# One copy of the K transposes addressed through a register, and PV in two column tiles of 64, in a one-core decode kernel

## The chip, the cores and the metric

The kernel runs on one core of one Trainium2 chip. The metric is the device time of one execution in microseconds. The kernel before takes 196.64 us, the median of three runs (196.57 to 196.75).

## The reference

Four sequences each decode one token. After a layer norm, the sum of three terms is written out: the input, an attention with its output projection, and a SwiGLU feed-forward.

```python
W = 4096                                   # the last 4096 positions of the cache
q = (xn @ wq), 32 heads of 128
k, v = the last W rows of 8 cached heads, each used by 4 query heads
scores = einsum("bhqd,bhkd->bhqk", q, k) * 128 ** -0.5
o = einsum("bhqk,bhkd->bhqd", softmax(scores), v) @ wo
out = x + o + (silu(xn @ w_gate) * (xn @ w_up)) @ w_down
```

There are 4 sequences, 8 cached heads, 16 query columns per cached head (4 sequences times 4 query heads), and 16384 rows of K and of V per cached head. One cached head of K, or of V, is 4 MB in bf16.

## The kernel before, in words

The work on the cache is a loop of eight passes, one per cached head, and a ninth, short one. K and V each have two buffers of 4 MB in SBUF, `KB[0]`, `KB[1]` and `VB[0]`, `VB[1]`; a head's parity chooses the buffer. A buffer holds 128 blocks of 128 by 128.

In pass j, TensorE does the following for head j-1.

- **Transposes** (`transposes`, line 415): 128 blocks of K are turned, eight to a PSUM bank and a group. The three banks `ps_kt0` to `ps_kt2` are used in turn. Each group (number n, 0 to 15) is copied to SBUF (`kT`) by VectorE (line 335, ten groups) or ScalarE (line 268, the groups 4, 7, 8, 11, 12 and 14). A group waits until the bank is free, which the semaphore `s_ev[n - 3]` tells.
- **Scores** (line 424): each turned block is the stationary operand, and 16 columns of q move through it. The results of all 128 blocks fill the four banks `ps_s`. The program goes: transposes 0 to 7, scores 0 to 3, transposes 8 to 11, scores 4 to 7, transposes 12 to 15, scores 8 to 15.
- **Sums of the previous head's exponentials** (line 515), then a transpose (line 519) of the column maxima that VectorE has reduced from the four banks (lines 339 to 365).
- **PV of the previous head** (`pv`, line 433): two blocks of the probabilities P (32 columns) are the stationary operand, and two blocks of V (256 columns) move. Four such products go to four column tiles of 32, that is, to four strips of 32 PSUM partitions in `ps_o`. Of each product only the two diagonal pieces of 16 by 128 are meant; the others are computed and left unused.
- **Shift** (line 532): four products subtract the maxima from the scores in place. ScalarE then takes the exponentials (line 271).
- **Fold** (line 536): VectorE has copied `ps_o` to SBUF (line 347), and fp32 products with a 0/1 matrix (`fold`) add the strips' pieces up. VectorE multiplies the result by the reciprocal of the sums (line 349) and so makes a head's output, and signals `s_nm`.

The maxima, the exponentials and the copies lie on VectorE and ScalarE, and the PV of a head runs one pass after its scores.

TensorE's program is a loop with branches. Three transposes sections and the PV section exist twice, once for each parity (`by_parity`), since the address of a K or V buffer is a constant in them. TensorE's sequencer (the part that reads the program) executes branches, register arithmetic and some waits itself and hands weight loads and products on to the array's queue. Where an address depends on a register, it is worked out by an instruction of its own, shown as FUSED_REGOPS in the profile and as ISA in the program's order. Before the change there is such an instruction at line 424, one ahead of each of three groups of scores, since all products of a group read the same q.

All transfers of K, V and the weights are issued by SyncE on one queue in a fixed order: the weights of q, gate and up, K0, K1, V0, then K2, V1, K3, V2 and so on to V7, then the weights of the down and output projections. The load of K for head r waits until the transposes of head r-2 are done (line 230, signal `s_tr[15]`), the load of V for head r until PV of pass r is done (line 235, signal `s_pv`).

After the ninth pass the tail (`t_tail`, line 554) transposes the heads' outputs, multiplies by the two projections' weights (lines 566, 574 and 586) and writes the result.

Of the kernel before, what the change touches and what calls it, by code (L numbers as in the profile page):

```python
# [3 lines left out]
BF16 = mybir.dt.bfloat16  # L4
FP32 = mybir.dt.float32
ALU = mybir.AluOpType
ACT = mybir.ActivationFunctionType
AX = mybir.AxisListType


def bass_parallel_sum__sliding_block_cached__swiglu_ffn__decode_kernel(
# [12 lines left out]
    B, _, D = A_x.shape  # L24
    _, HKV, Sk, Dh = A_k_cache.shape
# [6 lines left out]
    NT = W * B // 128  # L32
# [6 lines left out]
    CQ = B * REP  # L39
# [8 lines left out]

    sb = nc.alloc_sbuf_tensor
    sb("pad_to_512", [128, (-nc.sbuf_base) % 512 // 2], BF16)  # L50
    KB = [sb("kbuf%d" % s, [128, NT, Dh], BF16) for s in range(2)]
    VB = [sb("vbuf%d" % s, [128, NT, Dh], BF16) for s in range(2)]
    WG = sb("wg_sb", [128, NC, F], BF16)
    WU = sb("wu_sb", [128, NC, F], BF16)
    WD = WG[:].rearrange("p c n -> p (c n)").rearrange("p (t n) -> p t n", n=D)
    WO = KB[0][:].rearrange("p t d -> p (t d)").rearrange("p (j n) -> p j n", n=D)
    WQ = VB[1][:].rearrange("p t d -> p (t d)").rearrange("p (c n) -> p c n", c=NC)

    X = sb("x_sb", [B, D], BF16)
# [8 lines left out]
    P = sb("p", [128, NT, CQ], BF16)  # L68
# [8 lines left out]
    mask = sb("mask", [128, CQ], FP32)  # L77
    nrm = sb("nrm", [48, 1], FP32)
    Dsh = sb("dsh", [128, CQ], BF16)
    o4 = sb("o4", [128, 256], FP32)  # L80
    dsum = sb("dsum", [128, CQ], FP32)
    rden = sb("rden", [128, CQ], FP32)
    OT = sb("oT", [128, HKV + 1, CQ], BF16)
# [6 lines left out]
    ident = sb("ident", [128, 128], BF16)  # L90
# [2 lines left out]
    I48 = sb("i48", [48, CQ], FP32)  # L93
    Lsel = sb("lsel", [128, 128], BF16)
    fold = sb("fold", [128, 32], FP32)
    sel = sb("sel", [128, B, 128], BF16)
    quarter = sb("quarter", [128, 4], FP32)
    opf = sb("opf", [128, B, 32], FP32)
# [4 lines left out]
    ps_kt = [ps("ps_kt%d" % s, [128, 512], FP32) for s in range(3)]  # L103
    ps_O = ps("ps_o", [128, 512], FP32)
    kt_ps = [t[:].bitcast(BF16).rearrange("p (a b) -> p a b", b=128) for t in ps_kt]
    S_ps = [t[:].rearrange("p (t c) -> p t c", c=CQ) for t in ps_S]
    mx_ps = ps_kt[2][:, 0:128]
    mask_ps = ps_O[:, 0:CQ]
    o4_ps = ps_O[:, 0:256]
    dn_ps = ps_kt[0]  # L110
    ot_ps = ps_O[:, 288:288 + CQ]
    xT_ps = ps_S[0][:].bitcast(BF16)[:, 0:NC * B]
    gate_ps = ps_S[2]
    up_ps = ps_S[3]
# [11 lines left out]
    d_k = [sem("d_k%d" % g) for g in range(2)]  # L126
# [34 lines left out]
    s_oc = sem("s_oc")  # L161
    s_sl = sem("s_sl")
    s_nm = sem("s_nm")
# [20 lines left out]
    def kv_ap(cache, r):  # L184
        return cache[:, r, Sk - W:, :].rearrange("b (s t) d -> s b (t d)", t=NT)
# [41 lines left out]
    def run_sync(eng):  # L227
        def load_k(r):
            if r >= 2:
                eng.wait_ge(s_tr[NCH - 1], r - 1)  # L230
            eng.dma_start(KB[r % 2][:].rearrange("p t d -> p (t d)"), kv_ap(A_k_cache, r)).then_inc(d_k[r % 2], 16)

        def load_v(r):
            if r:
                eng.wait_ge(s_pv, r)
            eng.dma_start(VB[r % 2][:].rearrange("p t d -> p (t d)"), kv_ap(A_v_cache, r)).then_inc(d_v[r % 2], 16)

        eng.dma_start(WQ[:], wq_ap).then_inc(d_v[1], 16)
        eng.dma_start(WG[:], wg_ap).then_inc(d_wg, 16)
        eng.dma_start(WU[:], wu_ap).then_inc(d_wu, 16)  # L240
        load_k(0)
        load_k(1)
        load_v(0)
        for r in range(2, HKV):
            load_k(r)
            load_v(r - 1)
        load_v(HKV - 1)
        eng.dma_start(WD, wd_ap).then_inc(d_wd, 16)  # L248
        for q, (a, b) in enumerate(ROWS):
            if q == 0:  # L250
                eng.wait_ge(s_tr[NCH - 1], HKV - 1)
            eng.dma_start(WO[:, a:b, :], wo_ap[:, a:b, :]).then_inc(d_wo[q], 16)  # L252
        eng.wait_ge(s_y, 1)
        eng.dma_start(out_ap, y_ap).then_inc(d_out, 16)
        eng.wait_ge(d_out, 16)
# [20 lines left out]
    def run_vector(eng):  # L276
        me = bass.OrderedEngineSet([eng.engine])
        nx = nc.alloc_registers("v_r", engines=me)
# [23 lines left out]
        for h in (0, 32):  # L302
            eng.tensor_copy(I48[h:h + CQ, :], identf[h:h + CQ, h:h + CQ])
        eng.tensor_reduce(fold[:], ident[:].rearrange("p (g m) -> p m g", m=32), AX.X, ALU.add)
        eng.tensor_reduce(quarter[:], ident[:].rearrange("p (g m) -> p m g", m=4), AX.X, ALU.add)
        eng.tensor_copy(I4w[:].rearrange("p (b e) -> p b e", e=8)[:, :, 0], ident[0:B, 0:B])
        eng.wait_ge(s_q, 1)
# [33 lines left out]
        def sums(v, slot):  # L341
            eng.wait_ge(s_dn, v)
            eng.tensor_reduce(dsum[:], dn_ps[:].rearrange("p (t c) -> p c t", c=CQ), AX.X, ALU.add)  # L343
            eng.drain()
            eng.reciprocal(rden[:], dsum[:])
            eng.wait_ge(s_pv, v)
            eng.tensor_copy(o4[:], o4_ps).then_inc(s_oc, 1)  # L347
            eng.wait_ge(s_sl, v)
            eng.tensor_tensor(slot, ot_ps, rden[:], ALU.mult).then_inc(s_nm, 1)  # L349

# [33 lines left out]
        for q in range(1, 4):  # L384
            eng.drain()
            dst = opf[:] if q < 3 else OP[:].rearrange("p j (b e) -> p b j e", e=8)[:, :, :, 0]
            last = eng.scalar_tensor_tensor(dst, op_ps[:, :, q, :], quarter[:, q:q + 1], opf[:], ALU.mult, ALU.add)
# [6 lines left out]
    def run_tensor(eng):  # L394
        mm = eng.matmul
        me = bass.OrderedEngineSet([eng.engine])
# [4 lines left out]
        def now(reg, lo=1, hi=16 * HKV):  # L401
            return eng.snap(reg, min_val=lo, max_val=hi, donate=True)
# [1 line left out]
        def step(reg, by, op=ALU.add):  # L404
            nc.regs_alu(reg, reg, by, op=op)

        def transposes(g, a, b):
            if a == 0:
                eng.wait_ge(d_k[g], now(nk[g]))
            j = now(nx)  # L410
            for n in range(a, b):
                if n >= 3:
                    eng.wait_ge(s_ev[n - 3], j)
                for k in range(8):
                    last = eng.transpose(kt_ps[n % 3][:, k, :], KB[g][:, 8 * n + k, :], ident[:])  # L415
                last.then_inc(s_tr[n], 1)

        def scores(j, n):
# [9 lines left out]
                last.then_inc(s_sc[q], 1)  # L428

        def pv(e):  # L430
            for u in range(NT // 2):
                k = u % 4
                last = mm(o4_ps[32 * k:32 * k + 32, :], P[:, 2 * u:2 * u + 2, :].rearrange("p t c -> p (t c)"),  # L433
                          VB[e][:, 2 * u:2 * u + 2, :].rearrange("p t d -> p (t d)"),
                          start=(u < 4), stop=(u >= NT // 2 - 4), skip_group_check=True)
            last.then_inc(s_pv, 1)

        later = []
# [1 line left out]
        def by_parity(name, body):  # L440

            eng.br_lt(odd, 1, on_true=name + "_even", on_false=name + "_odd")
            later.append((name, body))
            with nc.body(name + "_even", valid_engines=me):
                body(0)
                nc.br(name + "_end", engines=me)
# [44 lines left out]

        with nc.body("t_pass", valid_engines=me):
            by_parity("t_a", lambda g: transposes(g, 0, 8))
        with nc.body("t_a_end", valid_engines=me):
            j = now(nx, 1, HKV)
            for n in range(0, 4):
                scores(j, n)
            by_parity("t_b", lambda g: transposes(g, 8, 12))  # L500
        with nc.body("t_b_end", valid_engines=me):
            j = now(nx, 1, HKV)
            for n in range(4, 8):
                scores(j, n)
            by_parity("t_c", lambda g: transposes(g, 12, 16))
        with nc.body("t_c_end", valid_engines=me):
            j = now(nx, 1, HKV)
            for n in range(8, 16):
                scores(j, n)
            nc.br("t_values", engines=me)  # L510
        with nc.body("t_values", valid_engines=me):
            j = now(nx)
            for q in range(NB):
                eng.wait_ge(s_xp[q], j)
                last = mm(dn_ps[:], ones[:], P[:, q * TB:(q + 1) * TB, :].rearrange("p t c -> p (t c)"),  # L515
                          start=(q == 0), stop=(q == NB - 1))
            last.then_inc(s_dn, 1)
            eng.wait_ge(s_cm, j)
            eng.transpose(mx_ps, mxd[:], identf[:]).then_inc(s_mt, 1)  # L519
            eng.wait_ge(s_nm, j)  # L520

            def turn(g):
                eng.wait_ge(d_v[1 - g], eng.snap(nk[g], min_val=16, max_val=16 * HKV))
                step(nk[g], 16)
                pv(1 - g)

            by_parity("t_p", turn)
        with nc.body("t_p_end", valid_engines=me):
            j = now(nx)
            eng.wait_ge(s_dd, j)  # L530
            for q in range(NB):
                mm(S_ps[q], Lsel[:], bc(Dsh[:], TB), start=False, stop=True,  # L532
                   skip_group_check=True).then_inc(s_sh[q], 1)
            eng.wait_ge(s_oc, j)
            for e in range(2):
                last = mm(ot_ps, o4[:, 128 * e:128 * e + 128], fold[:, 16 * e:16 * e + 16],  # L536
                          start=(e == 0), stop=(e == 1), skip_group_check=True)
            last.then_inc(s_sl, 1)
            nc.br("t_step", engines=me)
        with nc.body("t_step", valid_engines=me):  # L540
# [85 lines left out]
```

## Time and profile before

| what | value |
|---|---|
| median of three runs | 196.64 us |
| the profiled execution, whole | 196.87 us |
| its span in the profile | 195.4 us |
| PE busy (TensorE products) | 155.1 us (79%), 2903 instructions |
| PEld busy (weight loads) | 120.8 us (62%), 2912 |
| DVE (VectorE) busy | 115.3 us (59%), 220 |
| ACT (ScalarE) busy | 68.9 us (35%), 86 |
| packets of the main DMA queue | 97.1% of 16 engines' time, 81.01 MB |
| transposes, line 415 | 1024, busy 72.4 us |
| scores, line 424 | 1024, busy 29.4 us |
| PV, line 433 | 576, busy 18.8 us |

The span is what lies between the first and the last instruction of the execution; the whole has 1.5 us around it. The busy time of a group is the union of its instructions, so overlapping products count once. The "chain" goes back from the last instruction, at each step to what released it, and gives start, length, engine, tile and line. The "windows" give the busy time of each engine in a stretch and the clock that was granted to TensorE, 1.00 being full. PEldq marks what TensorE's sequencer executed itself; such instructions are not counted as busy.

### The profile page before, as it was taken

To read this page: it belongs to the slowest core of one execution; us is meant where nothing else is said; L and a number is where in the kernel's file an instruction comes from. 1 tells how busy PE (TensorE), PEld (TensorE's weight loads), DVE (VectorE), ACT (ScalarE), POOL (GpSimd) and SP (SyncE) were. 2 spreads that over 40 slices of the span, in tenths; PEclk is the share of its full clock that TensorE was granted. 3 is DMA by queue.
4 is the path that set the end of the run, shared out by engine and by line. 5 is a ranking of instruction groups with operands and counts; after the bars stand their busy time and mean duration, and the time that the engine had idled before them with its cause. 6 is when DMAs were issued, how large, how long until landed. Compare 5 with 4: busy or idle time off the path is not lost.

```text
span 195.4 us, 6505 instructions
## 1 busy us (share of the span) xinstructions
PE 155.1 (79%) x2903; PEld 120.8 (62%) x2912; DVE 115.3 (59%) x220; ACT 68.9 (35%) x86; POOL 9.2 (5%) x27
## 2 busy tenths in 40 slices
PE   0038935997999899899989989998699879987653
PEld 0012105985788679778867968886598758955311
DVE  5642373666486766758676676867276747672501
ACT  2003100470447056444706634560447046603001
POOL 7820000000000000000000000000000000000000
PEclk9999996698799999999999999999889999999968
DMA  6999999999999999999999999999999999999991
GB/s 216 429 438 432 459 429 436 433 429 426 426 429 426 429 431 436 443 429 429 436 429 429 429 429 429 429 429 429 436 429 436 429 436 429 429 429 398 419 401 52
DMA packets 3633, 81.09 MB, mean 415 GB/s; under 512 B 424, under 2 KB 556, under 8 KB 940
## 3 DMA queue, kind: packets, MB, share of 16 engines
q1 hardware_dynamic: 3620, 81.01, 97.1%
q8 instruction: 4, 0.07, 0.1%
q14 instruction: 1, 0.01, 0.0%
q10 hardware_dynamic: 8, 0.00, 0.0%
HBM read 81.01 MB, written 0.00 MB: 415 GB/s over the span
## 4 chain that ended last, share of the span: by engine, by line
DMA 45%; PE 39%; ACT 7%; DVE 3%; issue 2%; SPq 2%; DVEq 0%
DMA kbuf<-in_A_k_cache_dram 28%; PE ps_kt L415 21%; DMA kbuf<-in_A_wo_dram 17%; PE ps_s L424 9%; ACT kT L268 7%; PE ps_o L433 6%; PE ps_s L532 2%; DVE mxb L339 2%; PE ps_kt L519 1%; PE ps_o L536 1%; SPq L252 1%; DVE mx L362 1%; DVE mxd L364 0%; DVE kT L335 0%; SPq L248 0%
## 5 line engine op out<-in xcount | busy, mean ns | idle before, releaser
L415 PE MATMUL ps_kt<-ident,kbuf 128*128 128x128 bf16 x1024 | 72.4, 227 | 9.5 <-DMA kbuf<-in_A_k_cache_dram 5.9
L415 PEld LDWEIGHTS ps_kt<-ident,kbuf 128*128 128x128 bf16 x1024 | 61.9, 102 | 16.8 <-ACT kT L268 6.4
L335 DVE COPY kT<-ps_kt 128x1024 bf16<-128x1024 bf16 x80 | 52.2, 687 | 20.3 <-PE ps_kt L415 19.5
L268 ACT COPY kT<-ps_kt 128x1024 bf16<-128x1024 bf16 x48 | 47.8, 1013 | 44.5 <-PE ps_kt L415 44.5
L271 ACT ACTIVATE p<-ps_s 128x512 bf16<-128x512 f32 x32 | 16.5, 604 | 46.1 <-PE ps_s L532 46.1
L339 DVE TENSOR_REDUCE mxb<-ps_s 128x16 f32<-128x512 f32 x32 | 22.1, 692 | 13.3 <-PE ps_s L424 11.6
L424 PE MATMUL ps_s<-qT,kT 128*128 x1024 | 29.4, 169 | 0.0
L424 PEld LDWEIGHTS ps_s<-qT,kT 128*128 128x128 bf16 x1024 | 27.8, 96 | 0.3
L433 PE MATMUL ps_o<-vbuf,p 128*32 128x256 bf16 x576 | 18.8, 287 | 1.3 <-DMA vbuf<-in_A_v_cache_dram 0.8
L433 PEld LDWEIGHTS ps_o<-vbuf,p 128*32 128x32 bf16 x576 | 16.1, 101 | 4.2 <-issue 3.4
L532 PE MATMUL ps_s<-dsh,lsel 128*128 128x512 bf16 x36 | 9.4, 381 | 0.0
L515 PE MATMUL ps_kt<-p,ones 128*128 128x512 bf16 x27 | 7.6, 379 | 0.9 <-ACT p L271 0.2
L467 PE MATMUL ps_s<-vbuf,xnT 128*32 128x512 bf16 x32 | 3.6, 629 | 5.0 <-DMA vbuf<-in_A_wq_dram 5.0
L519 PE MATMUL ps_kt<-identf,mxd 128*128 128x128 f32 x9 | 3.0, 328 | 5.3 <-DVEq L365 5.3
L343 DVE TENSOR_REDUCE dsum<-ps_kt 128x16 f32<-128x512 f32 x9 | 6.2, 692 | 1.5 <-PE ps_kt L515 1.3
L349 DVE TENSOR_TENSOR oT<-ps_o,rden 128x16 f32 (+1 forms) x9 | 1.6, 175 | 8.9 <-PE ps_o L536 8.9
L519 PEld LDWEIGHTS ps_kt<-identf,mxd 128*128 128x128 f32 x9 | 1.3, 140 | 8.4 <-DVEq L365 8.4
L536 PEld LDWEIGHTS ps_o<-fold,o 128*128 128x128 f32 x36 | 5.4, 190 | 1.3
L347 DVE COPY o<-ps_o 128x256 f32<-128x256 f32 x9 | 3.8, 425 | 3.8 <-PE ps_o L433 3.2
L574 PE MATMUL ps_s<-kbuf,oP 128*32 128x512 bf16 x22 | 2.8, 623 | 3.8 <-DMA kbuf<-in_A_wo_dram 3.8
L457 PE MATMUL ps_s<-ident,xn 4*128 4x4 bf16 x4 | 0.3, 166 | 6.6 <-DVE xn L297 6.6
L274 ACT COPY part<-ps_s 64x512 f32<-64x512 f32 x1 | 0.6, 580 | 13.4 <-PE ps_s L574 13.4
(92 smaller groups left out, 71.7 us busy)
## 6 DMA issues: line engine op xcount, KB each, us to landing
kbuf<-in_A_k_cache_dram SPq DMA_DIRECT2D x8, 4096.0 KB, 24.3
vbuf<-in_A_v_cache_dram SPq DMA_DIRECT2D x8, 4096.0 KB, 26.2
vbuf<-in_A_wq_dram SPq DMA_DIRECT2D x1, 4096.0 KB, 12.1
kbuf<-in_A_wo_dram SPq DMA_DIRECT2D x1, 2048.0 KB, 29.9
wg_sb<-in_B_w_gate_dram SPq DMA_DIRECT2D x1, 1792.0 KB, 16.0
wu_sb<-in_B_w_up_dram SPq DMA_DIRECT2D x1, 1792.0 KB, 19.8
wg_sb<-in_B_w_down_dram SPq DMA_DIRECT2D x1, 1792.0 KB, 25.6
kbuf<-in_A_wo_dram SPq DMA_DIRECT2D x1, 896.0 KB, 33.0
```

The source lines that it names most:

```text
L268: eng.copy(KT[n % 8][:], kt_ps[n % 3]).then_inc(s_ev[n], 1)
L271: eng.activation(P[:, q * TB:(q + 1) * TB, :], S_ps[q], ACT.Exp, scale=SCALE).then_inc(s_xp[q], 1)
L335: eng.tensor_copy(KT[n % 8][:], kt_ps[n % 3]).then_inc(s_ev[n], 1)
L339: eng.tensor_reduce(mxb[:, q, :], S_ps[q].rearrange("p t c -> p c t"), AX.X, ALU.max)
L343: eng.tensor_reduce(dsum[:], dn_ps[:].rearrange("p (t c) -> p c t", c=CQ), AX.X, ALU.add)
L415: last = eng.transpose(kt_ps[n % 3][:, k, :], KB[g][:, 8 * n + k, :], ident[:])
L424: last = mm(S_ps[q][:, 8 * (n % 4) + k, :], KT[n % 8][:, k, :], QT[:, bass.ds(j, 1), :, :].rearrange("p o b h -> p (o b h)"), start=(n % 4 ...
L433: last = mm(o4_ps[32 * k:32 * k + 32, :], P[:, 2 * u:2 * u + 2, :].rearrange("p t c -> p (t c)"), VB[e][:, 2 * u:2 * u + 2, :].rearrange(" ...
L515: last = mm(dn_ps[:], ones[:], P[:, q * TB:(q + 1) * TB, :].rearrange("p t c -> p (t c)"), start=(q == 0), stop=(q == NB - 1))
L519: eng.transpose(mx_ps, mxd[:], identf[:]).then_inc(s_mt, 1)
L532: mm(S_ps[q], Lsel[:], bc(Dsh[:], TB), start=False, stop=True, skip_group_check=True).then_inc(s_sh[q], 1)
L536: last = mm(ot_ps, o4[:, 128 * e:128 * e + 128], fold[:, 16 * e:16 * e + 16], start=(e == 0), stop=(e == 1), skip_group_check=True)
```

## The change

K's two buffers become one tensor with an index 0 or 1, and the transposes stand once in the program. Each one's K address is worked out from the register `odd`, which changes between 0 and 1 at the end of each pass. Only the wait for K's arrival still exists for each parity. PV now takes four blocks of P (64 columns) as the stationary operand and four blocks of V (512 columns) as the moving one, alternating between two column tiles of 64 partitions. `ps_o` is therefore filled to its 512 columns, VectorE's copy of it is 512 wide, and the fold is four products with a new 0/1 matrix, `fold4`, instead of two. The fold's result moves from `ps_o` to a free part of `ps_kt2`. For that reason the third group of transposes now waits for `s_nm` (the product of VectorE that reads the fold's result), and the wait for `s_nm` stands ahead of the maxima's transpose instead of behind it.

```diff
-    KB = [sb("kbuf%d" % s, [128, NT, Dh], BF16) for s in range(2)]
+    KBA = sb("kbuf", [128, 2, NT, Dh], BF16)
+    KB = [KBA[:, s] for s in range(2)]
...
-    o4 = sb("o4", [128, 256], FP32)
+    o4 = sb("o4", [128, 512], FP32)
...
+    fold4 = sb("fold4", [128, 64], FP32)
...
-    o4_ps = ps_O[:, 0:256]
+    o4_ps = ps_O
...
-    ot_ps = ps_O[:, 288:288 + CQ]
+    ot_ps = ps_kt[2][:, 256:256 + CQ]
...
+        eng.tensor_reduce(fold4[:], ident[:].rearrange("p (g m) -> p m g", m=64), AX.X, ALU.add)
...
-        def transposes(g, a, b):
-            if a == 0:
-                eng.wait_ge(d_k[g], now(nk[g]))
+        def transposes(a, b):
             j = now(nx)
+            g = eng.snap(odd, min_val=0, max_val=1)
             for n in range(a, b):
+                if n == 2:
+                    eng.wait_ge(s_nm, j)
                 if n >= 3:
                     eng.wait_ge(s_ev[n - 3], j)
                 for k in range(8):
-                    last = eng.transpose(kt_ps[n % 3][:, k, :], KB[g][:, 8 * n + k, :], ident[:])
+                    last = eng.transpose(kt_ps[n % 3][:, k, :],
+                                         KBA[:, bass.ds(g, 1), 8 * n + k, :].rearrange("p o d -> p (o d)"), ident[:])
                 last.then_inc(s_tr[n], 1)
...
         def pv(e):
-            for u in range(NT // 2):
-                k = u % 4
-                last = mm(o4_ps[32 * k:32 * k + 32, :], P[:, 2 * u:2 * u + 2, :].rearrange("p t c -> p (t c)"),
-                          VB[e][:, 2 * u:2 * u + 2, :].rearrange("p t d -> p (t d)"),
-                          start=(u < 4), stop=(u >= NT // 2 - 4), skip_group_check=True)
+            for u in range(NT // 4):
+                k = u % 2
+                last = mm(o4_ps[64 * k:64 * k + 64, :], P[:, 4 * u:4 * u + 4, :].rearrange("p t c -> p (t c)"),
+                          VB[e][:, 4 * u:4 * u + 4, :].rearrange("p t d -> p (t d)"),
+                          start=(u < 2), stop=(u >= NT // 4 - 2), skip_group_check=True)
             last.then_inc(s_pv, 1)
...
         with nc.body("t_pass", valid_engines=me):
-            by_parity("t_a", lambda g: transposes(g, 0, 8))
-        with nc.body("t_a_end", valid_engines=me):
+            by_parity("t_k", lambda g: eng.wait_ge(d_k[g], now(nk[g])))
+        with nc.body("t_k_end", valid_engines=me):
+            transposes(0, 8)
             j = now(nx, 1, HKV)
             for n in range(0, 4):
                 scores(j, n)
-            by_parity("t_b", lambda g: transposes(g, 8, 12))
-        with nc.body("t_b_end", valid_engines=me):
-            j = now(nx, 1, HKV)
+            transposes(8, 12)
             for n in range(4, 8):
                 scores(j, n)
-            by_parity("t_c", lambda g: transposes(g, 12, 16))
-        with nc.body("t_c_end", valid_engines=me):
-            j = now(nx, 1, HKV)
+            transposes(12, 16)
             for n in range(8, 16):
                 scores(j, n)
...
+            eng.wait_ge(s_nm, j)
             eng.wait_ge(s_cm, j)
             eng.transpose(mx_ps, mxd[:], identf[:]).then_inc(s_mt, 1)
-            eng.wait_ge(s_nm, j)
...
-            for e in range(2):
-                last = mm(ot_ps, o4[:, 128 * e:128 * e + 128], fold[:, 16 * e:16 * e + 16],
-                          start=(e == 0), stop=(e == 1), skip_group_check=True)
+            for e in range(4):
+                last = mm(ot_ps, o4[:, 128 * e:128 * e + 128], fold4[:, 16 * e:16 * e + 16],
+                          start=(e == 0), stop=(e == 3), skip_group_check=True)
```

How the instructions of TensorE move is seen at two places. The first is the start of a pass: the branch by parity, the wait for K and the first transposes, before the change. `kbuf` is K, `ident` the identity matrix, `ps_kt` the PSUM bank.

```order
L442 COMPARE_AND_BRANCH
L415 MATMUL ps_kt<-ident,kbuf 128x128 [waits d_k0]
L415 MATMUL ps_kt<-ident,kbuf 128x128 x23
L415 MATMUL ps_kt<-ident,kbuf 128x128 [waits s_ev0]
L415 MATMUL ps_kt<-ident,kbuf 128x128 x7
```

The same place after the change, with its line numbers moved by a few:

```order
L447 COMPARE_AND_BRANCH
L451 UNCONDITIONAL_BRANCH [waits d_k0]
L412 ISA
L419 MATMUL ps_kt<-ident,kbuf 128x128
L419 ISA
L419 MATMUL ps_kt<-ident,kbuf 128x128
L419 ISA
L419 MATMUL ps_kt<-ident,kbuf 128x128
```

An instruction of register arithmetic (ISA) now stands ahead of every one of the 128 transposes of a pass, three operations in each, and the waits for K and for free banks moved from the transposes to the branch and to such instructions.

The second place is PV and what follows it up to the fold, before the change:

```order
L442 COMPARE_AND_BRANCH [waits s_nm]
L405 REGISTER_ALU [waits d_v1]
L433 MATMUL ps_o<-vbuf,p 32x256 x64
L446 UNCONDITIONAL_BRANCH
L532 MATMUL ps_s<-dsh,lsel 128x512 [waits s_dd]
L532 MATMUL ps_s<-dsh,lsel 128x512 x3
L536 MATMUL ps_o<-fold,o 128x16 [waits s_oc]
L536 MATMUL ps_o<-fold,o 128x16
```

and after it:

```order
L447 COMPARE_AND_BRANCH
L408 REGISTER_ALU [waits d_v1]
L438 MATMUL ps_o<-vbuf,p 64x512 x32
L451 UNCONDITIONAL_BRANCH
L535 MATMUL ps_s<-dsh,lsel 128x512 [waits s_dd]
L535 MATMUL ps_s<-dsh,lsel 128x512 x3
L539 MATMUL ps_kt<-fold,o 128x16 [waits s_oc]
L539 MATMUL ps_kt<-fold,o 128x16 x3
```

PV has half as many products, each with twice the columns on both sides, and the fold twice as many products.

More of the change, by code (lines that the diff above doesn't have):

```diff
@@ L55, in bass_parallel_sum__sliding_block_cached__swiglu_ffn__decode_kernel @@
     WD = WG[:].rearrange("p c n -> p (c n)").rearrange("p (t n) -> p t n", n=D)
-    WO = KB[0][:].rearrange("p t d -> p (t d)").rearrange("p (j n) -> p j n", n=D)
+    WO = KB[0].rearrange("p t d -> p (t d)").rearrange("p (j n) -> p j n", n=D)
     WQ = VB[1][:].rearrange("p t d -> p (t d)").rearrange("p (c n) -> p c n", c=NC)
@@ L230, in load_k @@
                 eng.wait_ge(s_tr[NCH - 1], r - 1)
-            eng.dma_start(KB[r % 2][:].rearrange("p t d -> p (t d)"), kv_ap(A_k_cache, r)).then_inc(d_k[r % 2], 16)
+            eng.dma_start(KB[r % 2].rearrange("p t d -> p (t d)"), kv_ap(A_k_cache, r)).then_inc(d_k[r % 2], 16)
         def load_v(r):
@@ L346, in sums @@
             eng.wait_ge(s_pv, v)
-            eng.tensor_copy(o4[:], o4_ps).then_inc(s_oc, 1)
+            eng.tensor_copy(o4[:], o4_ps[:]).then_inc(s_oc, 1)
             eng.wait_ge(s_sl, v)
```

## The prediction

> **What bounds the kernel now.** I read the page's busy slices first, then the chain of waits through one pass, then the windows.
>
> ```profile
> DMA  6999999999999999999999999999999999999991
> 54.50:179.50 125.00, 112.61 (x2329) 94.80 (x2337) 83.67 (x162) 56.29 (x70) 0.00 (x0) 0.99 1.00 430
> kbuf<-in_A_k_cache_dram SPq DMA_DIRECT2D x8, 4096.0 KB, 24.3
> vbuf<-in_A_v_cache_dram SPq DMA_DIRECT2D x8, 4096.0 KB, 26.2
> PE ps_kt L415 <- DMA kbuf<-in_A_k_cache_dram: 5.9, 3, 2.9
> ```
>
> The transfers never stop (share 1.00, 430 GB/s), so the sum of bytes sets the end. A pass needs 2 x 4096 KB, 8.39 MB, which is 19.5 us. TensorE starts late, because K0 is fourth in the queue, and then runs its passes faster than the data come; it waits for K only three times. This is one undisturbed pass in the chain:
>
> ```profile
> 86.85 4.31 PE ps_kt L415 x64
> 91.16 0.86 PE ps_s L424 x32
> ...
> 94.21 0.82 PE ps_s L424 x32
> ...
> 97.21 1.61 PE ps_s L424 x64
> ...
> 98.85 0.69 DVE mxb L339
> ...
> 100.22 0.33 PE ps_kt L519
> ...
> 100.67 1.93 PE ps_o L433 x64
> 102.61 0.97 PE ps_s L532 x4
> 103.58 0.35 PE ps_o L536 x4
> ```
>
> From 86.85 to 103.93 the pass takes 17.08 us: transposes 4.31 and twice 2.19 (from one score group's end to the next one's start, the waits for copies included), scores 0.86, 0.82 and 1.61, VectorE's maxima 1.40 (from the scores' end at 98.82 to 100.22), their transpose with what follows 0.45, PV 1.93, shift 0.97, fold 0.35. So TensorE has 2.4 us a pass to spare against the transfers. Whatever raises its pass by more turns the bound over.
>
> **The change part by part: the register arithmetic.** Each transpose gets an instruction that the sequencer executes itself, 128 in a pass, one behind the other. The trace has that instruction, and a pair of others that shows what lies between two of them (durations in ns, least, median and most, then the first and last start in us):
>
> ```profile
> L424 PEldq FUSED_REGOPS  x24: 46/46/46, 37.0 to 169.4; - x24
> ...
> L405 PEldq ALU_OP  x2: 32/34/36, 51.9 to 52.0; - x2
> ```
>
> ```profile
> 70.03 0.06 DVEq L349
> ...
> 70.13 0.07 DVE oT L349
> ```
>
> FUSED_REGOPS with three operations takes 46 ns, and the new ones have three too. Two neighbouring ALU_OPs take 34 ns each and start 0.1 us apart, so about 66 ns lie between. VectorE shows the same with the very instruction: 0.06 us of arithmetic, and its engine begins 0.10 us after the arithmetic began. I take 46 + 66 = **112 ns per transpose** and nothing for handing over the weight load and the product: score products, whose q address is also a register's, run at 0.82/32 = 26 ns a pair.
>
> Today the array turns 64 blocks in 4.31 us, 67 ns a block with the copies' waits. From both sides: if the arithmetic hid wholly behind the array and the copies, the price would be 67 ns (nothing gained or lost). If the weight load that takes its address from the register needs one more handover, 178 ns. The value is nearest to the ALU pair, because the alternation makes every arithmetic instruction wait for the previous one's end. The sequencer can run ahead of the array, but that helps only while the array has other work: 128 x 112 ns = 14.3 us a pass instead of 4.31 + 2.19 + 2.19 = 8.7. The copies are no limit any more: a group now takes 0.90 us. The waits of the transposes for banks and for s_nm, now on sequencer instructions, cost nothing in addition, since at this pace three groups, 2.7 us, lie between two uses of a bank.
>
> **Run-ahead at the scores.** While the array does 32 scores, the sequencer goes on to the next transposes.
>
> ```profile
> L442 PEldq COMPARE_BRANCH  x1: 223/223/223, 57.3 to 57.3; - x1
> 57.05 0.81 PE ps_s L424 x32
> ```
>
> The branch behind a group of scores begins at 57.3 and the scores end at 57.86, so about 0.3 us of each of the two inner groups is covered: 0.55 instead of 0.86 and 0.82. The last 64 scores stay 1.61, with 0.2 ahead of them for the sequencer's own two instructions. The parity branches that vanish (this one takes 0.22 us) were covered by the array's scores and save nothing; if the array were idle, they would be 0.2 us each.
>
> **PV.** Four products of 256 columns side by side take 1.93/16 = 0.12 us and do eight blocks of V. After the change, two of 512 columns do eight blocks. The shift's products of 512 columns take 0.97/4 = 0.24 us, of which a stream needs 0.22. So 16 pairs x 0.22 + 0.13 of start = 3.65 us, 1.72 more, if the two tiles overlap as the four do. Without overlap it is 32 x 0.22, 7 us, which over nine passes would make the end 275; if the array were no bound at all, 1.93. The four narrow tiles overlap in this trace, so I take 3.65.
>
> **Fold and copy.**
>
> ```profile
> L347 DVE COPY o<-ps_o 128x256 f32<-128x256 f32 x9 | 3.8, 425 | 3.8 <-PE ps_o L433 3.2
> ```
>
> Four pieces take 0.35 us; eight take about 0.75. The copy of 512 columns is priced by VectorE's reduction of a bank of 512 (0.69 at 98.85): 0.69 instead of 0.43, still under the shift's 0.97, so nothing. Behind the fold's wait for it stand the sequencer's steps and branches of the next pass; they end about when the longer fold does. If that cover were gone, they would cost 0.3 us. The new 0/1 matrix costs VectorE one reduction before K0 arrives: nothing. The wait for s_nm ahead of the maxima's transpose asks for a product done a whole pass earlier: nothing.
>
> **The sum.** New pass: shift 0.97, fold 0.75, transposes 14.34, scores 0.55 + 0.55 + 1.81, maxima 1.40, their transpose 0.45, PV 3.65: **24.5 us**, above the transfers' 19.5. TensorE becomes the bound from the first pass on.
>
> ```profile
> 31.32 6.59 PE ps_kt L415 x64
> ...
> 45.47 0.69 DVE mxb L339
> ...
> 48.04 3.33 PE ps_o L433 x62
> ```
>
> And from the timeline of the end:
>
> ```profile
> 174.95 1.04 PE L532 MATMUL ps_s<-dsh,lsel 128*128 128x512 bf16 x4
> ...
> 184.53 0.77 DVE L387 SCALAR_TENSOR_TENSOR oP<-ps_s,quarter,opf 128x128 bf16<-128x128 f32 x1
> ...
> 187.99 2.82 PE L574 MATMUL ps_s<-kbuf,oP 128*32 128x512 bf16 x22 [3.80 <-DMA kbuf<-in_A_wo_dram]
> ```
>
> K0 is there at 31.3 as before. The first PV ends at 31.3 + 14.34 + 1.10 + 1.81 + 2.6 (maxima and their transpose, here 45.45 to 48.04) + 3.65 = 54.8, against 51.37 (48.04 + 3.33). Seven more passes of 24.5 end the eighth PV at 226.3, against 174.95. From there to the span's end it takes 195.4 - 174.95 = 20.45 now. The waits for late data fall away, as the last loads start at the seventh PV (201.8) and their 9.9 MB take 23 us: the output weights 187.99 - 185.30 = 2.7, 1.5 of L574's 2.82 (22 products at 0.24 for four need 1.3), and about 1.1 for V7 and the last weights, an estimate, 5.3 in all. The last PV, fold and copy add 1.72 + 0.4 + 0.27. That leaves 17.5, so the span is 243.8. The profiled execution took 196.87 with a span of 195.4, 1.5 around it: **245 us**. The median of the runs, 196.64, lies 0.2 below the profiled one, which is nothing here. Each nanosecond of the 112 moves the end by 128 x 8 ns = 1.02 us.
>
> **The rivals.** (a) *The arithmetic is hidden and PV alone costs.* The pass is 17.08 + 1.72 + 0.40 = 19.2, just under the transfers, but it also eats TensorE's lead: the first PV ends at 51.37 + 2.1 = 53.5, and 53.5 + 7 x 19.2 + 17.5 + 1.5 = **207 us**. For it speaks that the sequencer runs ahead at L442; against it the ALU pair.
>
> (b) *The clock falls.* With a block every 112 ns, the array streams only about half the time during transposes.
>
> ```profile
> 31.30:37.30 6.00, 5.98 (x57) 5.99 (x58) 3.41 (x5) 1.01 (x1) 0.00 (x0) 0.50 1.02 434
> 37.40:47.50 10.10, 8.42 (x204) 7.56 (x203) 6.58 (x11) 4.96 (x5) 0.00 (x0) 1.00 1.01 433
> 47.60:51.00 3.40, 3.33 (x61) 2.54 (x64) 1.68 (x5) 0.00 (x0) 0.00 (x0) 0.50 0.90 386
> ```
>
> At a granted 0.50, after VectorE's long first chain, PV took 3.33 instead of 1.93. If that comes in every pass, PV goes from 3.65 to 6.3, in nine passes 24 us more, **269 us**. The transposes, paced by the sequencer, would not care (6.59/64 = 103 ns at 0.50). Against it: the passes with 1.4 us of VectorE's chain in each kept 0.99 on average (the first window above). The Trainium skill, "TensorE: Matmul & The Clock Gate", Part 4 on transposes in PE mode, says that transposes do not count as busy for the gate and full rate does not engage for them. The trace disagrees for dense ones: the clock rose to 1.00 by 37.4 us with only transposes run, from 31.3 on. By that rule this rival would be the likeliest; by the row it is open at half the density.
>
> (c) *A transpose needs two handovers*, 178 ns: 245 + 66 x 1.02 = **312 us**. Against it speak the score pairs.
>
> (d) *Not slower.* One mechanism: the array and the sequencer are not the limit of PV and transposes. PV's two wide tiles stream as the four narrow ones do, at 1.93, and the arithmetic stays under 67 ns a block. Then the pass is 17.5 and the transfers bound as now, **196.6 us**. It decides up to a pass of about 17.7, where eight passes have used up the tail's 5.3 us of waits (5.3/8 = 0.66 over 17.08). Against it: the shift's 0.24 for 512 columns.
>
> **How the numbers follow.** Forecast 0.64, (a) 0.12, (b) 0.12, (c) 0.07, (d) 0.05. The predicted time is the forecast's, 245. The range 222 to 276 is a price of 90 to 142 ns per transpose, takes in (b), and leaves out (a), (c) and (d) and little else: 0.2 or a bit more. A measurement of this kernel tells 0.2% from no change. Faster only out of (d), where two parity branches a pass go: 0.02; same 0.03; slower 0.95.
>
> **What would show it.** The chain should be TensorE's nearly throughout, with K's transfers gone from it after the first; DMA slices under 9 between the passes; passes of 24 to 25 us; FUSED_REGOPS 1024 and more at 46 ns, and groups of 64 transposes at 7.2 us instead of 4.31, the array idle between them for no wait that shows; PV of 32 products in 3.6 us. Wrong would be: 64 transposes in under 5 us (a), PV in 6 us at a clock of 0.50 (b), 64 transposes in 11 us (c), or a DMA row still full at 9 (d).

## The result and the profile after

The changed kernel takes **266.88 us**, the median of four runs (265.5 to 267.22), against 196.69 us (196.57 to 196.94) for the kernel before on the same chip. The ratio is 1.3553, with a 95% interval of 1.3503 to 1.3603. The forecast was 245 us with a range of 222 to 276: the direction and the mechanism came out, the size by 22 us too small. The profiled execution took 267.02 us with a span of 265.8.

From the page of the changed kernel (the span, busy time of the engines, the granted clock and the transfers in 40 slices, the main queue, the chain by engine and by line, and the group of the transposes):

```profile
span 265.8 us, 7015 instructions
...
PE 238.5 (90%) x2651; PEld 161.4 (61%) x2660; DVE 121.1 (46%) x221; ACT 69.6 (26%) x86; POOL 8.9 (3%) x27
...
PEclk9999779899999999899999997999799979997999
DMA  8999999799729971999099909990899104999200
...
q1 hardware_dynamic: 3620, 81.01, 72.3%
...
PE 84%; DMA 11%; DVE 2%; issue 1%; SPq 1%; DVEq 0%
...
L419 PE MATMUL ps_kt<-ident,kbuf 128*128 128x128 bf16 x1024 | 131.8, 229 | 3.6 <-DMA kbuf<-in_A_k_cache_dram 3.2
```

The bound has turned over. Before, the DMA row was full from the second slice to the last but one; now it falls to 2, 1 or 0 once in most passes, and the queue's packets fill 72.3% of the span instead of 97.1%. The chain is TensorE's for 84% of the span; K's transfer holds 11%, which is the first one.

The waits of SyncE ahead of the loads of K show the same from the other side (for each: who ended it, us, times, the longest), first before, then after:

```profile
SPq L231 <- PE ps_kt L415: 95.2, 6, 39.7
```

```profile
SPq L233 <- PE ps_kt L419: 142.0, 6, 45.7
```

Those of before were long too, but hidden, because the queue still held other loads (its share was 97.1%). Now the queue runs dry.

One pass in the chain of the changed kernel (start, us, what), from its first transposes to those of the next pass, and, set ahead and behind, the end of the first PV, the PV just before that pass, and the end of the eighth PV:

```profile
57.09 0.43 PE ps_o L438 x4
...
108.13 3.86 PE ps_o L438 x28
...
113.89 8.40 PE ps_kt L419 x64
...
122.30 0.96 PE ps_s L429 x32
123.26 3.87 PE ps_kt L419 x32
127.13 0.85 PE ps_s L429 x32
127.97 3.81 PE ps_kt L419 x32
131.79 1.70 PE ps_s L429 x64
...
133.51 0.69 DVE mxb L342
...
135.45 3.64 PE ps_o L438 x32
139.09 0.97 PE ps_s L535 x4
140.06 0.88 PE ps_kt L539 x8
140.94 0.68 PE ps_kt L419 x5
...
248.19 0.43 PE ps_o L438 x4
```

The pass takes 27.05 us (113.89 to 140.94). Its 128 transposes hold 8.40 + 3.87 + 3.81 = 16.08 us, against 4.31 + 2 x 2.19 = 8.69 before. The chain shows no wait within the transposes' rows: a product is in flight all the time, since the page gives each 229 ns (227 before) and one starts every 126 ns on average (16.08/128). The forecast had expected the array to be shown idle between them. The same 1024 transposes, each shown as long as before, now fill 131.8 us instead of 72.4 because they start farther apart; PE's busy time alone does not tell that the array is fed too slowly.

### The profile page after: what moved, and what is told of

It is laid out like the page before. It is cut to its first block, busy times and chain, and to the rows that moved or that the text cites. A ratio compares the mean times of both kernels' runs of the same rounds, so it can differ in the third digit from the quotient of the medians.

```text
span 265.8 us, 7015 instructions
## 1 busy us (share of the span) xinstructions
PE 238.5 (90%) x2651; PEld 161.4 (61%) x2660; DVE 121.1 (46%) x221; ACT 69.6 (26%) x86; POOL 8.9 (3%) x27
## 3 DMA queue, kind: packets, MB, share of 16 engines
q1 hardware_dynamic: 3620, 81.01, 72.3%
## 4 chain that ended last, share of the span: by engine, by line
PE 84%; DMA 11%; DVE 2%; issue 1%; SPq 1%; DVEq 0%
PE ps_kt L419 49%; PE ps_o L438 13%; DMA kbuf<-in_A_k_cache_dram 11%; PE ps_s L429 11%; PE ps_kt L518 4%; PE ps_s L535 3%; PE ps_kt L539 3%; PE ps_kt L523 1%; PE ps_s L577 1%; DVE mxb L342 1%; DVE oP L390 0%; SPq L242 0%; DVE opf L390 0%; DVE part L393 0%; PE ps_s L589 0%
## 5 line engine op out<-in xcount | busy, mean ns | idle before, releaser
L419 PE MATMUL ps_kt<-ident,kbuf 128*128 128x128 bf16 x1024 | 131.8, 229 | 3.6 <-DMA kbuf<-in_A_k_cache_dram 3.2
L419 PEld LDWEIGHTS ps_kt<-ident,kbuf 128*128 x1024 | 96.4, 96 | 36.7 <-issue 4.1
L338 DVE COPY kT<-ps_kt 128x1024 bf16<-128x1024 bf16 x80 | 55.3, 692 | 64.0 <-PE ps_kt L419 64.0
L438 PE MATMUL ps_o<-vbuf,p 128*64 128x512 bf16 x288 | 34.4, 393 | 0.4 <-issue 0.4
L438 PEld LDWEIGHTS ps_o<-vbuf,p 128*64 128x64 bf16 x288 | 17.4, 114 | 15.2 <-issue 4.2
L350 DVE COPY o<-ps_o 128x512 f32<-128x512 f32 x9 | 6.2, 692 | 18.1 <-PE ps_o L438 18.1
L518 PE MATMUL ps_kt<-p,ones 128*128 128x512 bf16 x27 | 11.5, 549 | 1.6 <-issue 1.4
L539 PEld LDWEIGHTS ps_kt<-fold,o 128*128 128x128 f32 x72 | 8.7, 191 | 2.8 <-DVE o L350 2.8
L539 PE MATMUL ps_kt<-fold,o 128*128 128x16 f32 x72 | 9.4, 262 | 0.0
L518 PEld LDWEIGHTS ps_kt<-p,ones 128*128 128x128 bf16 x36 | 3.6, 119 | 4.4 <-issue 3.3
```

What stands on the lines that cost most here:

```text
L338: eng.tensor_copy(KT[n % 8][:], kt_ps[n % 3]).then_inc(s_ev[n], 1)
L350: eng.tensor_copy(o4[:], o4_ps[:]).then_inc(s_oc, 1)
L419: last = eng.transpose(kt_ps[n % 3][:, k, :], KBA[:, bass.ds(g, 1), 8 * n + k, :].rearrange("p o d -> p (o d)"), ident[:])
L438: last = mm(o4_ps[64 * k:64 * k + 64, :], P[:, 4 * u:4 * u + 4, :].rearrange("p t c -> p (t c)"), VB[e][:, 4 * u:4 * u + 4, :].rearrange(" ...
L539: last = mm(ot_ps, o4[:, 128 * e:128 * e + 128], fold4[:, 16 * e:16 * e + 16], start=(e == 0), stop=(e == 3), skip_group_check=True)
```

## The experiments

All were run beside the kernel before, which took 196.69 or 196.73 us (medians) in them.

**The registers alone.** PV, the copy, the fold and their waits stay as before; K's place is chosen by a register and the transposes stand once in the program, as in the change. The lines below show only the address.

```diff
-    KB = [sb("kbuf%d" % s, [128, NT, Dh], BF16) for s in range(2)]
+    KBA = sb("kbuf", [128, 2, NT, Dh], BF16)
+    KB = [KBA[:, s] for s in range(2)]
...
+            g = eng.snap(odd, min_val=0, max_val=1)
...
-                    last = eng.transpose(kt_ps[n % 3][:, k, :], KB[g][:, 8 * n + k, :], ident[:])
+                    last = eng.transpose(kt_ps[n % 3][:, k, :],
+                                         KBA[:, bass.ds(g, 1), 8 * n + k, :].rearrange("p o d -> p (o d)"), ident[:])
```

> The K transposes are addressed through the register as in the changed kernel; PV, the copy and the fold are those of before. Theory (the sequencer's register arithmetic sets the pace, 129 ns a transpose on average in the changed kernel's trace): a pass is the changed kernel's 27.3 less 1.7 for PV and 0.4 for the fold, 25.2; end about 248 us. FUSED_REGOPS start 124 ns apart, with a longer step in every eighth. Rival (PV and the clock that falls around it are the larger part): under 225 us. Rival (the new place of the fold's result and the wait for s_nm hold the transposes): the transposes return to 4.3 us for 64 and the time to about 197.

Measured: 248.32 us (247.91 to 248.8), ratio 1.2632 (1.2611 to 1.2654). A pass in its chain:

```profile
104.27 1.91 PE ps_o L434 x64
...
107.81 8.41 PE ps_kt L415 x64
...
117.18 3.87 PE ps_kt L415 x32
...
121.90 3.88 PE ps_kt L415 x32
...
129.29 1.80 PE ps_o L434 x57
```

The transposes cost here what they cost in the whole change, 16.16 us a pass. So neither the wide PV nor the moved waits slow them; the register addressing, with one copy of the transposes, does so by itself and makes the kernel 51.6 us slower.

**The wide PV alone.** Transposes by parity with constants as before; PV, copy, fold and the two waits for `s_nm` as in the change.

```diff
-            for u in range(NT // 2):
-                k = u % 4
-                last = mm(o4_ps[32 * k:32 * k + 32, :], P[:, 2 * u:2 * u + 2, :].rearrange("p t c -> p (t c)"),
...
+            for u in range(NT // 4):
+                k = u % 2
+                last = mm(o4_ps[64 * k:64 * k + 64, :], P[:, 4 * u:4 * u + 4, :].rearrange("p t c -> p (t c)"),
```

> The transposes exist once for each parity as before; PV in two column tiles of 64, the copy of 512 columns, the fold of four products and the wait for s_nm are those of the changed kernel. Theory (PV costs 1.7 us a pass more and the fold 0.4 on a path that has 0.66 us a pass to spare over the whole run, though 2.4 against the transfers' rate): a pass of 19.2 to 19.4, end 207 us. Rival (a pass still below the transfers' 19.5 is hidden): 196.7 us. Rival (the two tiles don't run side by side): PV 7 us, end above 225.

Measured: 205.07 us (203.79, 203.92, 206.22 and 206.53; why they lie in two pairs is open), ratio 1.0448 (1.0378 to 1.0517). From the chain of the execution of 203.92:

```profile
104.76 3.64 PE ps_o L437 x32
...
109.38 0.88 PE ps_kt L540 x8
110.26 4.23 PE ps_kt L419 x64
...
123.86 3.64 PE ps_o L437 x32
```

PV takes 3.64 us instead of 1.93, as costed. The pass is 19.10 us (104.76 to 123.86), the next one 19.38, still under the transfers' 19.5, and yet the kernel is 8.4 us slower: the longer passes use up TensorE's lead first, and what is left of them shows at the end. On top of the registers the same edit costs 266.88 - 248.32 = 18.6 us, because there no transfer covers it: 1.73 of PV and 0.53 of fold would make 20.3 in nine passes, and the mean of the seven passes between the ends of the first and the eighth PV grew by 2.13 us (25.17 to 27.30). That is why the two parts, 51.6 and 8.4 us, do not add up to the 70.2 of the whole change.

**A register addition ahead of each transpose.** The kernel before with its constant addresses, and one addition to a register that nothing reads until the end. It tells whether the sequencer's instruction as such costs the time, or the address that comes from a register.

```diff
                 for k in range(8):
+                    step(spare, nx)
                     last = eng.transpose(kt_ps[n % 3][:, k, :], KB[g][:, 8 * n + k, :], ident[:])
```

> The kernel before with one register addition ahead of every transpose, whose result no address uses; K's addresses stay constants. Theory (what costs is that the sequencer executes an instruction between two transposes, not the address): 36 ns of arithmetic and the same 78 ns around it, 114 to 119 ns a transpose; 64 transposes in about 7.5 us, end about 244 us. Rival (a weight load whose address comes from a register is what is slow): 64 transposes in 4.3 us, end 196.7 us.

Measured: 243.57 us (243.41 to 243.72), ratio 1.2382 (1.2357 to 1.2407). From its chain, and from the view of the line that holds the addition (durations in ns, least, median, most, and the first and last start):

```profile
105.81 7.81 PE ps_kt L416 x64
...
114.82 3.81 PE ps_kt L416 x32
```

```profile
L405 PEldq ALU_OP  x34: 34/34/34, 133.1 to 137.1; - x34
```

An addition that no product uses costs 46.9 us. The address is not what is dear; an instruction of the sequencer between two products is. Not all of it lies in the transposes: the passes of one parity take 23.6 to 23.7 us between the ends of PV, those of the other 25.1 to 25.8. The same view of the line of the changed kernel:

```profile
L419 PEldq FUSED_REGOPS  x32: 46/46/46, 143.0 to 147.0; - x32
```

32 starts in 4.0 us are 129 ns from one to the next (4.0/31), 34 additions in 4.0 us are 121 (4.0/33). In the single starts of the trace most steps are 124 ns (115 for the addition) and one in eight is 165 (156). So between the end of one such instruction and the start of the next lie 124 - 46 = 78 ns, or 115 - 34 = 81, plus 41/8 = 5 for the long steps. The forecast had 66.

**Half of the groups by register.** K's place comes from the register in groups 0 to 7, from constants in groups 8 to 15, with the code still there for each parity.

```diff
+            v = eng.snap(odd, min_val=0, max_val=1)
...
-                    last = eng.transpose(kt_ps[n % 3][:, k, :], KB[g][:, 8 * n + k, :], ident[:])
+                    src = KB[g][:, 8 * n + k, :]
+                    if n < 8:
+                        src = KBA[:, bass.ds(v, 1), 8 * n + k, :].rearrange("p o d -> p (o d)")
+                    last = eng.transpose(kt_ps[n % 3][:, k, :], src, ident[:])
```

> The kernel before with the first 64 transposes of each pass addressed through the register and the other 64 by constants, in code for each parity; PV as before. Theory (129 ns for each transpose that follows an instruction of the sequencer, the copies' pace for the others): 64 transposes take 8.3 us instead of 4.3, a pass 21.0 instead of 17.1, end 216 to 217 us. Rival (the price depends on how long the stretch of such transposes is, since the sequencer's lead in the array's queue covers the first ones): a pass under 19.5 and under 205 us.

Measured: 220.13 us (219.4 to 221.29), ratio 1.12 (1.1156 to 1.1244), some 3.5 us over the expectation. From its chain:

```profile
50.39 3.52 PE ps_o L438 x49
...
116.70 1.93 PE ps_o L438 x64
...
119.96 8.35 PE ps_kt L420 x64
...
129.26 0.48 PE ps_kt L420 x8
...
137.75 1.91 PE ps_o L438 x64
...
141.09 8.40 PE ps_kt L420 x64
...
159.32 1.93 PE ps_o L438 x64
```

The 64 transposes by register take the full 8.35 us, and the first eight of the others run at 0.48, 60 ns a block. The price belongs to the instructions and ends with them. The miss is in the passes: 21.05 us (116.70 to 137.75) is what was expected for all, but every other pass takes 21.57 (to 159.32). Between the ends of the first and the eighth PV (53.91 and 203.86) the seven passes take 2.6 us more than 7 x 21.05, and 1.6 come from the first PV, which ran 3.52 instead of 1.93 at a granted clock of 0.50.

**Every second transpose by register, and every fourth.** The edit is that of the last one, with another condition. It separates two readings of the 129 ns: a fixed cost on every register-addressed transpose, or a pace of the sequencer that is hidden as soon as the array has enough queued.

```diff
-                    if n < 8:
+                    if k % 2 == 0:
```

> The kernel before with K in one tensor and every second transpose addressed through the register, the others by constants, in code for each parity. Theory (a pace set by the slower of two: the sequencer at 124 ns for two transposes, 62 to 66 ns each, against the array's 56 and the copies' 75): 64 transposes stay near 4.4 us and the end between 196.6 and 199 us. Rival (each register-addressed transpose costs its 61 ns more wherever it stands): 512 x 0.061 us = 31 us more, 228 us.

Measured: 197.22, 198.51, 201.06 and 201.76 us. The spread is too wide for a ratio of use, and two of the four lie above the expected 199; why is open. The profiled execution took 198.51. From its page and its chain:

```profile
DMA  6999999999999999999999999999999999999980
...
PE 63%; DMA 15%; ACT 9%; DVE 6%; issue 5%; SPq 1%; DVEq 0%; ACTq 0%
...
106.88 1.93 PE ps_o L438 x64
...
110.13 4.66 PE ps_kt L420 x64
...
124.65 1.91 PE ps_o L438 x64
...
143.65 1.36 PE ps_o L438 x41
```

64 transposes take 4.66 us with 32 such instructions among them, 146 ns for two. The passes are 17.77 (106.88 to 124.65) and 19.00 us (to 143.65), under the transfers' 19.5 again, and the DMA row is full nearly to the end. The chain, though, holds no transfer after K0, whose load is the 15%: TensorE's own work ends last now, at a span of 197.3 us against 195.4 before, and the two limits lie close together. A fixed cost would have left half of the 51.6 us; between 0.5 and 5.1 of them are there, 1.8 in the profiled execution. In the single starts the sequencer's instructions lie 124 ns apart here too wherever they follow each other without a stop, with two weight loads and two products between them instead of one of each: what is between two of them doesn't grow with the number of products that the sequencer hands over.

The last one has `k % 4 == 0` in that place.

> As e7_every_second, with the register's address at every fourth transpose. Theory (the pace is the slower of sequencer and array, and one handover covers any number of products behind it): 124/4 = 31 ns a transpose of the sequencer's time, under the array's 56; transposes as before, 196.6 to 197.4 us. Rival (a share of each handover always reaches the array): 256 x 0.061 us = 16 us more, 212 us; or half of e7_every_second's 3 us, 198.2 us.

Measured: 197.67 us (197.42 to 198.23), ratio 1.0047 (1.0033 to 1.0061). From its chain:

```profile
107.02 1.93 PE ps_o L438 x64
...
110.28 1.44 PE ps_kt L420 x24
...
111.73 3.02 PE ps_kt L420 x40
...
124.19 1.91 PE ps_o L438 x64
```

The transposes take 4.47 us, the pass 17.17, both within 0.2 of before; every other pass takes 17.95 between the ends of PV, which the transfers' 19.5 cover. The time lies between the expected 197.4 and the 198.2 of the second rival. The 0.9 us over the kernel before aren't in the passes: the median span of its five runs is 195.6 us against 195.4, and 1.5 to 2.3 us lie around the span instead of 1.2 to 1.4. What that is stays open.

**The place of the fold's result.** The registers alone, plus the fold's result in the third transposes bank and the waits for `s_nm` that go with it. It prices the waits that had been costed at nothing.

```diff
-    ot_ps = ps_O[:, 288:288 + CQ]
+    ot_ps = ps_kt[2][:, 256:256 + CQ]
...
+                if n == 2:
+                    eng.wait_ge(s_nm, j)
```

> As e1_registers_only, with the fold's result in ps_kt2, the wait for s_nm ahead of the third group of transposes and ahead of the maxima's transpose, as in the changed kernel. Theory (these waits are for work that is long done): the same 248.3 us as e1_registers_only, within 1 us. Rival (the third group waits for VectorE's product at each pass's start): 0.3 to 0.6 us a pass, 251 to 253 us.

Measured: 249.07 us (248.93 to 249.25), ratio 1.266 (1.2639 to 1.2681). That is 0.75 us over the registers alone, 0.1 us a pass: close to nothing, as costed.

## Why the prediction was right, and where it was too small

**That the bound turns over** was right: passes far above the transfers' 19.5 us, the chain TensorE's, K's transfer in it once, DMA slices down to 0 between loads.

**The price of a transpose, 112 ns, is the step that failed.** The 46 ns of the instruction were right. The 66 ns between two instructions were read from a pair of additions with no product between them. With a weight load and a product to hand on, 78 to 81 lie there, and one step in eight is longer, so the pace is 129 ns. The step "nothing for handing over the weight load and the product" should have had 12 to 15 ns. By the prediction's own 1.02 us for each nanosecond, 17 ns more are 17.4 of the 22 us. The row could have told that it was not of the same kind; the range, 90 to 142 ns, held the value.

**Run-ahead at the scores** had the right size in another row. The scores did not shrink to 0.55: they take 0.96, 0.85 and 1.70, together 3.51, where 3.29 and 0.2 for the sequencer's own instructions make 3.49. Instead, the two inner groups of 32 transposes take 3.87 and 3.81 where 32 x 129 is 4.13. That is 0.26 and 0.32 saved against 0.31 and 0.27 credited; that the sequencer works ahead during the scores fits this, though no run singled it out. The first group of a pass takes 0.14 more than 64 x 129. So the pass of 27.05 us against 24.47 splits into 2.18 for the price of the transposes, 0.15 less run-ahead than credited, 0.02 for the scores, 0.13 for the fold, 0.11 for the maxima and their transpose.

**PV** was right: 3.64 us against 3.65. Two tiles of 64 columns overlap as the four of 32 do: a pair of products takes 3.64/16 = 0.23 us, where one product of the shift, also of 512 columns, takes 0.24. **The fold** took 0.88 instead of 0.75, and **shift, copy and waits** cost what was said.

**From the pass to the end.** The first PV ends at 57.52 (57.09 + 0.43) instead of 54.8, with more to pay in the first pass. Between there and the end of the eighth PV at 248.62 lie seven passes of 27.3 us, 0.25 above the one shown. The tail took 17.2 us (265.8 - 248.62) against 17.5: that the waits for late data vanish was right. (The last loads are 9984 KB, 10.2 MB instead of the forecast's 9.9, which changes nothing here.) So 2.7 + 7 x 2.8 - 0.3 = 22.0 us is the whole miss.

**Rival (a), hidden arithmetic with PV alone to pay,** fell for the change, but the run with the wide PV alone is its measurement: 205.07 us where it said 207, with a pass of 19.1 where it said 19.2.

**Rival (b), the falling clock,** came in part. The clock row above shows sevens in many passes, and the windows around one of them show how long it lasts (columns: us; busy time and instructions of PE, weight loads, VectorE, ScalarE and GpSimd; granted clock; DMA share; GB/s):

```profile
54.10:105.20 51.10, 50.12 (x573) 36.37 (x571) 23.26 (x42) 16.28 (x20) 0.00 (x0) 1.00 0.72 309
105.30:108.60 3.30, 3.07 (x42) 1.62 (x41) 2.19 (x6) 0.00 (x0) 0.00 (x0) 0.50 0.88 318
108.70:159.80 51.10, 50.15 (x579) 36.42 (x577) 23.09 (x42) 16.27 (x20) 0.00 (x0) 1.00 0.72 308
```

A fall lasts some 3.4 us, here through the chain of the maxima and into PV, and the clock is back at 1.00 while PV still runs. PV took 3.86 there (108.13 in the chain) instead of 3.64. The rival's price of 24 us assumed nine PVs wholly at half speed. In five of the seven passes behind the first PV a fall reaches into PV; they take 27.25 to 27.45 us between the ends of PV, the two others 27.10 and 27.16. From these an estimate of what the falls cost is some 1.3 us in all. Compare the clock rows, first of the registers alone:

```profile
PEclk9999869999997999997999997999997999998899
```

then of the wide PV alone:

```profile
PEclk9999975999999999999999999999999999999999
```

of every second transpose by register:

```profile
PEclk9999975798899999999999999999999999999999
```

and of the kernel before:

```profile
PEclk9999996698799999999999999999889999999968
```

Where a transpose comes every 129 ns, the clock falls again and again; where one comes every 66 to 73 ns (4.23/64, 4.66/64), it stays at full after the first passes, but for one fall in the kernel before (its two eights, behind a wait for K) and its tail, although nearly half of a pass is transposes. The Trainium skill, "TensorE: Matmul & The Clock Gate", Part 4, says that full rate doesn't engage for transposes, as they don't count as busy in the same way. The dense ones here do not bear that out, and for the spread ones it says too much: the window from 108.70 shows 1.00 through a whole pass with 16.08 us of them. How busy the array has to be was not tried by itself.

**Rival (c), two handovers at 178 ns,** fell: 129. **Rival (d), not slower,** fell with the transposes and with PV each: either part alone is slower, by 51.6 and 8.4 us.

**A better version** was not found. With every fourth transpose by register the span is within 0.2 us of before; the transfers bound both (97.1% of the time before), so a shorter pass of TensorE has nothing to win until fewer bytes move.

## What to carry to other kernels

An address that a register gives is cheap only where few of the sequencer's instructions stand among the products: count the instructions that the sequencer itself executes, multiply by their pace from a trace in which products lie between them, and compare that with the array's pace for the work between two of them. If a loop with two buffers needs a new register address for each small product, code for each parity is cheaper, or an alternation with products at constant addresses. And two edits that each lengthen an engine's pass don't add up while the first is still partly covered: ask of each how much cover the other one leaves.

## What the runs showed of the hardware that was not expected

- Between two instructions that TensorE's sequencer executes itself lie 78 to 81 ns if products are handed on in between, and about 66 if none are (the pair of additions in the kernel before, 98 ns from start to start). It is the same for one weight load with its product (124 ns from start to start) and for two (124 ns).
- One step in eight is 41 ns longer, for the address arithmetic (165 against 124 ns) as for a plain addition (156 against 115). It goes by the count of these instructions: with two products a step instead of one it still comes every eighth of them. The cause is open.
- With code for each parity, passes alternate in length: 21.05 and 21.57 us with half of the groups by register, 17.77 and 19.00 with every second transpose, but also 17.14 and 17.95 with every fourth, 19.10 and 19.38 with the wide PV alone, and 16.87 and 17.08 in the kernel before. So it does not need the sequencer as the limit; it costs time where no transfer covers it. In the pass of 19.00 us the transposes' short groups take 0.60 to 0.66 us instead of 0.48 to 0.66, and 0.18 us for which the chain shows no wait stand ahead of each of the three groups of scores, none in the pass of 17.77. A branch by parity takes between 68 and 224 ns in the kernel before; whether that is the cause was not tried. With one copy of the transposes no such alternation stands out beside the falls of the clock (27.10 to 27.45 us in the change).
- With transposes 129 ns apart, a granted clock of 0.50 came in windows of some 3.4 us in most passes; with transposes 66 to 73 ns apart, once or not at all in the loop after its first passes.
